# Two GpSimd sums of a fused FFT and two-MLP kernel, issued at the end of earlier rounds

## The chip, the cores and the metric

The kernel runs on one core of one Trainium2 chip. The metric is the device time of one execution in microseconds (us). The core's engines run side by side, each through its own queue of instructions in order: TensorE (PE in the rows, its weight loads PEld), VectorE (DVE), ScalarE (ACT), GpSimd (POOL) and SyncE (SP), which issues most DMAs.

## The reference, cut to what matters

```python
X = np.fft.fft(np.fft.fft(x, axis=1), axis=2).real   # x: 8 x 3072 x 256
h = X.reshape(24576, 256) @ moe_w_in                 # 256 -> 2048
x2 = (h - np.tanh(h)) @ moe_w_out                    # 2048 -> 256
h2 = x2 @ moe2_w_in                                  # 256 -> 1024
e = np.exp(h2 - h2.max(-1)); solu = h2 * e / (e.sum(-1) + 1e-9)
ln = (solu - solu.mean(-1)) / np.sqrt(solu.var(-1) + 1e-6) * g_ln
out = ln @ moe2_w_out                                # 1024 -> 256
```

All of it is in float32. To multiply at TensorE's faster rate with nearly that precision, the kernel splits each operand into a rounded high part and the rest (low part), and makes three passes: high x high, high x low, low x high.

## The kernel before, in words

The transforms over the sequence come first (until about 165 us). The transform over the features is folded into the first weights. What then fills the time is a loop over 48 groups `n` of 512 output rows, with 16 rounds `j` each (`step = 16 n + j`); `m`, a chunk of 128 of the first layer's 2048 features, goes with a round. A round issues work of several ages, in an order that is written out by hand, and each engine executes its share in that order:

- `parity` (L879) makes h of chunk `m` on TensorE, `act_in` (L904, L912) finishes it on VectorE and takes tanh on ScalarE, `act_out` (L921) subtracts; the high part `gh` is rounded by ScalarE (L166) and the low part by GpSimd (`rest`, L169), two rounds after h. One chunk in four has its low part from VectorE instead. `o1` (L941), three rounds after h, multiplies `gh` by the second weights into x2 (`x2p`); its last two of six matmuls read the low part.
- After the last chunk of a group, in round 2 of the next, ScalarE copies x2 (transposed: features x rows) to `xb`: blocks A11, A12, A21, A22. The second layer's first product is made by a Strassen-like scheme of seven products, and so needs sums of blocks, which GpSimd makes in `sum_x2` (L957): S1 = A21 + A22, S2 = S1 - A11, S3 = A11 - A21, S4 = A12 - S2. Each is for both halves (128 rows each) of the group's row pairs.
- `split_x2` splits blocks into high (ScalarE, L166) and low parts (GpSimd, L169) in `xs`, half by half: A11 and A12 in round 3, S2 and S3 in round 5, A22, S1 and S4 in round 7 for the first half; in rounds 11, 13 and 15 for the second.
- `product` (L970) multiplies them into two banks, `bank_a` and `bank_b`. The product of S2 stands at the end of round 6 (second half: round 14): its three passes read the high part twice, and the low part of S2 last.
- The rest of the second layer follows over some 20 rounds: `block` (L992), `power` (L1007), `weigh` (L1016, on VectorE: u times e, both in SBUF), `square` (L1027), `scale` (L1035 to L1041, three small GpSimd instructions), `turn` (L1046, then a transpose through DRAM), `split_moved` (high part on ScalarE, low part `ut` on GpSimd, L169), `outp` (L1074, L1081), `scaled` and `store` (L1095). Two `weigh` fall in rounds 4 and 6, two in 12 and 14; `split_moved` falls in the even rounds.

Within a round the order is: `parity`, `act_in`, `lead`, `act_out` (with `rest` for `gh`), `layer2(step, "ahead")`, the block sums, `layer2(step, "early")` (with `split_moved`, then `split_x2`), `o1`, `layer2(step, "late")`, then weights of the first two groups, loads and sums for the next group.

So GpSimd's order is, in round 3: S1, S2, low part of A11 and A12; in round 4: `gh`, S3, `ut`; in round 5: `gh`, S4, low part of S2 and S3; in round 6: `gh`, then others.

Of the kernel before, what the change touches and what calls it, by code (L numbers as in the profile page):

```python
# [32 lines left out]
NG = B * GPB  # L33
# [106 lines left out]
def fft2_moe_moe_kernel(  # L140
# [559 lines left out]
    for q in range(NQ):  # L700
        b, j = divmod(q, NSJ)
# [73 lines left out]
    A11, A12, A21, A22, S1, S4, S2, S3 = range(8)  # L775
# [22 lines left out]
    def split_wi2(eng, b):  # L798
        split_halves(eng, wi2[:, b, 0], wi2[:, b, 1], whole_of(b))
# [152 lines left out]
    def sum_x2(b):  # L952
        a0, a1, op = {
            S1: (A21, A22, ALU.add), S2: (S1, A11, ALU.subtract),
            S3: (A11, A21, ALU.subtract), S4: (A12, S2, ALU.subtract),
        }[b]
        nc.gpsimd.tensor_tensor(out=xb[:, b], in0=xb[:, a0], in1=xb[:, a1], op=op)  # L957
# [9 lines left out]
    def product(p, bank, a, b, start=False):  # L967

        for q, (hx, hw) in enumerate(PASSES):
            nc.tensor.matmul(  # L970
                in_pairs(bank),
                xs[:, hx, xs_at[a]],
                in_turn(wi2[:, b, hw]),
                start=(start and q == 0),
                stop=(q == 2),
                skip_group_check=True,
            )

    def new_u(t):
        us[t] = (wk.tile([P, FF2], F32, tag="u", bufs=3, name=f"u{t}"), None)  # L980
        sts[t] = wk.tile([P, 12], F32, tag="st", bufs=8, name=f"st{t}")
        return us[t][0]

    def kept(t, f):
        nc.scalar.copy(out=us[t][0][:, f * HF : (f + 1) * HF], in_=bank_b)
# [27 lines left out]
    def weigh(t, h=None):  # L1013
        e, st = es.pop(t), sts[t]
        u = us[t][0]
        nc.vector.scalar_tensor_tensor(  # L1016
            out=u, in0=u if h is None else h, scalar=-1.0 if h is None else 1.0, in1=e,
            op0=ALU.mult, op1=ALU.mult, accum_out=st[:, 2:3],
        )
        us[t] = (u, e)  # L1020
# [72 lines left out]
    def store(t):  # L1093
        o = o2s.pop(t)
        nc.vector.scalar_tensor_tensor(  # L1095
            out=o, in0=pos.pop(t)[:, :D], scalar=sts.pop(t)[:, 10:11], in1=o, op0=ALU.mult, op1=ALU.add
        )
        us.pop(t)
        nc.sync.dma_start(out=out[t * P : (t + 1) * P, :], in_=o)
# [8 lines left out]
    def layer2(step, place):  # L1108

        works = {  # L1110
            "ahead": (
                (20, lambda p: store(2 * p + 1)),
                (24, lambda p: store(2 * p)),
                (2, lambda p: product(p, bank_a, A12, B21)),
                (4, lambda p: product(p, bank_b, S3, T3)),
                (6, lambda p: product(p, bank_b, A22, T4)),
                (1, lambda p: nc.scalar.copy(out=bank_b, in_=bank_a)),
                (3, lambda p: (new_u(2 * p), kept(2 * p, 1))),
            ),
            "early": (  # L1120
                (17, lambda p: outp(2 * p + 1, 0)),
                (19, lambda p: outp(2 * p + 1, 1)),
                (21, lambda p: outp(2 * p, 0)),
                (23, lambda p: outp(2 * p, 1)),
                (3, lambda p: block(2 * p, 0, bank_a, False, True)),
                (5, lambda p: block(2 * p + 1, 1, bank_a, True, True)),
                (6, lambda p: block(2 * p + 1, 0, bank_b, False, False)),
                (7, lambda p: block(2 * p, 1, bank_a, True, False)),
                (7, lambda p: power(2 * p + 1)),
                (8, lambda p: (power(2 * p), weigh(2 * p + 1))),  # L1130
                (9, lambda p: turn(2 * p + 1)),
                (10, lambda p: (weigh(2 * p), square(2 * p + 1), scale(2 * p + 1))),
                (12, lambda p: (square(2 * p), scale(2 * p), turn(2 * p))),
                (14, lambda p: split_moved(2 * p + 1, 0)),
                (16, lambda p: split_moved(2 * p + 1, 1)),
                (18, lambda p: split_moved(2 * p, 0)),
                (20, lambda p: split_moved(2 * p, 1)),
                (-1, lambda p: split_x2(p, A11, A12)),
                (1, lambda p: split_x2(p, S2, S3)),
                (3, lambda p: split_x2(p, A22, S4)),  # L1140
            ),
            "late": (
                (0, lambda p: product(p, bank_a, A11, B11, True)),
                (2, lambda p: product(p, bank_b, S2, T2)),
                (4, lambda p: product(p, bank_a, S1, T1, True)),
                (6, lambda p: product(p, bank_a, S4, B22)),
                (4, lambda p: (new_u(2 * p + 1), kept(2 * p + 1, 1))),
                (19, lambda p: scaled(2 * p + 1)),
                (23, lambda p: scaled(2 * p)),
            ),  # L1150
        }
        for back, work in works[place]:
            p = pair_at(step, back)
            if p is not None:
                work(p)
# [11 lines left out]
    for step in range(steps + 3):  # L1167
        n, j = divmod(step, NM)
        if step in at_ab:
            special(at_ab[step])  # L1170
        if 0 < step <= steps:
            parity(*divmod(step - 1, NM), 1)
        if step < steps:
            even(n, j)
        if 0 < step <= steps:
            act_in(*divmod(step - 1, NM))
        if step < steps:
            lead(n, j)
        lag = 3 if step < NM else 2
        for s in range(out_done, min(step - lag + 1, steps)):  # L1180
            act_out(*divmod(s, NM))
        out_done = max(out_done, min(step - lag + 1, steps))
        if step - 1 in wo2_at:
            split_wo2(wo2_at.index(step - 1), True)
        layer2(step, "ahead")
        if 0 < n < NG:
            for blk in {3: (S1, S2), 4: (S3,), 5: (S4,)}.get(j, ()):
                sum_x2(blk)
        layer2(step, "early")
        if NM <= step < steps + 2:  # L1190
            low_by_vector(*divmod(step - 2, NM))
        if step in at_o1:
            special(at_o1[step])
        if step in (NM, NM + 2):
            mean_wo2((step - NM) // 2)
        if step == NM + 2:
            nc.tensor.matmul(bank_b, wi2[:, B11, 0, :P], wi2[:, B11, 0], start=True, stop=True)
        s1 = step - 5 if step < NM else step - 3
        for s in (range(o1_done, min(s1 + 1, steps))):
            o1(*divmod(s, NM))  # L1200
        o1_done = max(o1_done, min(s1 + 1, steps))
        layer2(step, "late")
        if step in (3, 5, 7, 9):
            c, part = divmod((step - 3) // 2, 2)
            split_wo1(c + 2, wo1_raw[c + 2], slice(part * 2, part * 2 + 2))
        if step == NM:
            raw1.close()
            mv = pool(mv_stack, "mv", 2, side="right")
        if step in wi2_sums:
            sum_wi2(nc.vector, wi2_sums[step])  # L1210
        if step in wi2_splits:
            split_wi2(nc.gpsimd, wi2_splits[step])
        if step in (2, 3):
            load_wo2(step - 2)
        if step == 3:
            for k in range(2):
                load_wi2(k)
        if 8 <= step < NM:
            gain_wo2(step - 8)
        if step in (NM + 3, NM + 4):  # L1220
            center_wo2(step - NM - 3)
        if step in wo2_at:
            split_wo2(wo2_at.index(step), False)
        if step == NM + 12:
            nc.scalar.copy(out=pas, in_=pa)
        if step == NM + 20:
            special_out()
        if n == NG - 1 and j == 9:

            b12 = zp.tile([P, HF], F32, tag="zf", name="b12")  # L1230
            nc.sync.dma_start(out=b12, in_=wi2_d[0][:, HF:])
        if n == NG - 1 and j == 12:
            split_halves(nc.gpsimd, wt[0][:, 0, 0], wt[0][:, 1, 0], b12)
        if step == NM + 30:
            make_identity(nc, ident)
        if 1 <= n and n + 1 < NG:
            if j == 3:
                load_z(n + 1)
            for u in range(2):
                if j == 7:  # L1240
                    sum_z(n + 1, u, nc.gpsimd)
                if j == 11:
                    whole, hi, lo = by_half(n + 1, u)
                    rnd(hi, whole)
                    rest(nc.gpsimd, lo, whole, hi)
# [158 lines left out]
```

## Time and profile before

| | |
|---|---|
| median of 3 runs | 2728.41 us (2728.27 to 2728.82) |
| profiled execution | 2731.39 us |
| its span, first to last instruction | 2729.3 us |
| TensorE busy (matmuls) | 2650.9 us, 97% of the span |
| VectorE busy | 2200.1 us, 81% |
| ScalarE busy | 2035.8 us, 75% |
| GpSimd busy | 2084.7 us, 76% |
| mean granted TensorE clock | 0.997 |

A row of a timeline has the start, the duration, the engine, the line, the instruction with its output and inputs, and in brackets the idle time of the engine just before it, with what ended it. On GpSimd and TensorE the durations are rough; the distance from one start to the next, where the engine doesn't idle, is the better measure of what an instruction takes of its engine.

### The profile page before, as it was taken

The numbers are of one execution on the slowest core, as the hardware profiler recorded it, in microseconds if no ns is written. First come the engines' busy times: TensorE is split into PE (matmuls) and PEld (weight loads), VectorE is DVE, ScalarE is ACT, GpSimd is POOL, SyncE is SP. The second block draws the span as 40 slices with busy tenths as digits, with TensorE's granted clock in tenths as the row PEclk, the third lists the DMA queues.
The fourth block names the chain that finished last, engine by engine and source line by source line (L and its number), as shares of the span: only waits on it lengthen the run. The fifth ranks groups of instructions, "written<-read, shape, count | busy, mean of one in ns | idle before, by whom it ended". The sixth has DMA issues, their size and how long they took to land.

```text
span 2729.3 us, 47917 instructions
## 1 busy us (share of the span) xinstructions
PE 2650.9 (97%) x15073; PEld 2345.3 (86%) x15073; DVE 2200.1 (81%) x4389; ACT 2035.8 (75%) x3990; POOL 2084.7 (76%) x2309
## 2 busy tenths in 40 slices
PE   9999999999999999999999999999999999999998
PEld 6677888888888888888888888888888888888887
DVE  8977788888878888787877888878887788787885
ACT  3556777777777777777777777777777777777775
POOL 0047888888888888888888888888888888888874
PEclk9989999999999999999999999999999999999999
DMA  9951444444444443444444444344444444444441
GB/s 357 367 180 44 101 93 101 100 96 101 99 95 102 100 97 90 107 94 94 103 101 97 96 99 102 93 107 94 95 102 101 99 95 99 101 93 106 94 93 51
DMA packets 882652, 302.99 MB, mean 111 GB/s; under 512 B 788544, under 2 KB 844144, under 8 KB 879104
## 3 DMA queue, kind: packets, MB, share of 16 engines
q1 hardware_dynamic: 879792, 293.45, 43.9%
q10 hardware_dynamic: 2304, 6.42, 0.6%
q8 instruction: 120, 1.97, 0.3%
q14 instruction: 132, 1.08, 0.1%
q0 software_dynamic: 304, 0.07, 0.0%
HBM read 161.26 MB, written 138.60 MB: 110 GB/s over the span
## 4 chain that ended last, share of the span: by engine, by line
PE 74%; POOL 14%; DVE 5%; issue 4%; DMA 2%; ACT 1%; SPq 0%; POOLq 0%; DVEq 0%; ACTq 0%
PE x2p L941 29%; PE h L879 16%; PE po L1074 10%; PE bank_a L970 7%; PE bank_b L970 6%; PE po L1081 5%; POOL gh L169 5%; POOL xs L169 4%; POOL xb L957 3%; POOL ut L169 2%; DVE cv L452 1%; DVE pm L457 1%; DVE sm L447 1%; DMA tts<-tt 0%; DMA x<-xr 0%
## 5 line engine op out<-in xcount | busy, mean ns | idle before, releaser
L941 PE MATMUL x2p<-gh,wo 128*128 128x512 f32 x4608 | 1125.9, 380 | 1.4 <-POOL gh L169 1.4
L169 POOL TENSOR_TENSOR gh<-t,gh 128x512 fp32r<-128x512 f32 x584 | 812.7, 1392 | 257.2 <-ACT gh L166 243.9
L941 PEld LDWEIGHTS x2p<-gh,wo 128*128 128x128 f32 x4608 | 831.0, 190 | 116.2 <-POOL gh L169 10.6
L912 ACT ACTIVATE t<-h 128x512 f32<-128x512 f32 x762 | 453.5, 595 | 368.7 <-DVE h L904 298.5
L904 DVE SCALAR_TENSOR_TENSOR h<-asb,h 128x256 f32<-128x256 f32 x762 | 326.3, 428 | 458.5 <-PE h L879 452.3
L879 PEld LDWEIGHTS h<-zs,wt 128*128 128x128 f32 x4572 | 633.3, 191 | 49.0 <-DVE asb L897 2.9
L879 PE MATMUL h<-zs,wt 128*128 128x256 f32 x4572 | 643.0, 276 | 4.2 <-DVE asb L897 2.1
L1074 PE MATMUL po<-wo,ut 128*128 128x512 f32 x1528 | 522.2, 383 | 1.9 <-DVE o L1095 1.1
L169 POOL TENSOR_TENSOR ut<-um,ut 128x512 fp32r<-128x512 f32 x372 | 477.8, 1284 | 5.1 <-ACT ut L166 5.1
L166 ACT ACTIVATE gh<-t 128x512 fp32r<-128x512 f32 x584 | 370.0, 633 | 139.9 <-DVE t L921 137.0
L1081 PE MATMUL po<-wo,ut 128*128 128x256 f32 x1528 | 416.5, 273 | 0.0
L921 DVE TENSOR_TENSOR t<-h,t 128x512 f32<-128x512 f32 x578 | 395.2, 684 | 0.0
L169 POOL TENSOR_TENSOR xs<-xb,xs 128x256 fp32r<-128x256 f32 (+1 forms) x282 | 279.1, 990 | 133.9 <-ACT xs L166 101.2
L897 DVE SCALAR_TENSOR_TENSOR asb<-nb,wnu,h 128x256 f32<-128x256 f32 x762 | 363.5, 477 | 1.9 <-PE h L879 1.9
L1074 PEld LDWEIGHTS po<-wo,ut 128*128 128x128 f32 x1528 | 289.9, 190 | 32.9 <-DVE o L1095 1.6
L970 PE MATMUL bank_a<-wi,xs 128*128 128x512 f32 x1128 | 305.8, 380 | 1.9 <-POOL xs L169 1.1
L970 PE MATMUL bank_b<-wi,xs 128*128 128x512 f32 x846 | 242.1, 386 | 53.4 <-POOL xs L169 52.7
L1081 PEld LDWEIGHTS po<-wo,ut 128*128 128x128 f32 x1528 | 293.4, 192 | 0.2
L1016 DVE SCALAR_TENSOR_TENSOR u<-u,e 128x1024 f32<-128x1024 f32 x188 | 279.9, 1489 | 0.0
L970 PEld LDWEIGHTS bank_a<-wi,xs 128*128 128x128 f32 x1128 | 206.2, 189 | 28.2 <-POOL xs L169 1.7
L1046 DVE STREAM_TRANSPOSE tb<-u 128x1024 f32<-128x1024 f32 x186 | 229.7, 1235 | 0.0
L166 ACT ACTIVATE ut<-um 128x512 fp32r<-128x512 f32 x372 | 229.3, 616 | 0.0
(156 smaller groups left out, 3161.9 us busy)
## 6 DMA issues: line engine op xcount, KB each, us to landing
mv_d<-tb SPq DMA_DIRECT2D x186, 512.0 KB, 2.7
um<-mv_d SPq DMA_DIRECT2D x744, 128.0 KB, 3.8
out<-o SPq DMA_DIRECT2D x192, 128.0 KB, 1.7
x<-xr SPq DMA_DIRECT2D x23, 1024.0 KB, 10.6
zf<-z_d SPq DMA_DIRECT2D x64, 128.0 KB, 3.7
z_d<-zt ACTq DMA_DIRECT2D x16, 392.0 KB, 6.1
wi<-w_in SPq DMA_DIRECT2D x6, 1024.0 KB, 6.9
z_d<-zt SPq DMA_DIRECT2D x16, 384.0 KB, 9.6
```

The costliest lines, as they stand in the source:

```text
L166: nc.scalar.activation(out=o, in_=i, func=AF.Copy)
L169: eng.tensor_tensor(out=o, in0=i, in1=hi.bitcast(F32), op=ALU.subtract)
L879: nc.tensor.matmul(in_pairs(hs[n, m][:, 0]), wt[c][:, hw, u, o : o + P], in_turn(zs[:, hz, u]), start=(u == 0 and i == 0), stop=(i == 2), ...
L897: nc.vector.scalar_tensor_tensor(out=asb, in0=zg[n][1], scalar=wnu[:, m : m + 1], in1=hs[n, m][:, 0], op0=ALU.mult, op1=ALU.add)
L904: nc.vector.scalar_tensor_tensor(out=h[:, 1], in0=as_.pop((n, m)), scalar=2.0, in1=h[:, 0], op0=ALU.mult, op1=ALU.subtract)
L912: nc.scalar.activation(out=t, in_=h, func=AF.Tanh)
L921: nc.vector.tensor_tensor(out=g, in0=h, in1=t, op=ALU.subtract)
L941: nc.tensor.matmul(in_pairs(x2p[n][mt]), wo1[c][:, hw, k, mt * P : (mt + 1) * P], in_turn(gh[:, hg]), start=(m == 0 and i == 0), stop=(m = ...
L970: nc.tensor.matmul(in_pairs(bank), xs[:, hx, xs_at[a]], in_turn(wi2[:, b, hw]), start=(start and q == 0), stop=(q == 2), skip_group_check= ...
L1016: nc.vector.scalar_tensor_tensor(out=u, in0=u if h is None else h, scalar=-1.0 if h is None else 1.0, in1=e, op0=ALU.mult, op1=ALU.mult, a ...
L1074: nc.tensor.matmul(in_pairs(po), ut[:, 0, ks], wo2[:, k].rearrange("p h x n -> p (x n) h"), start=(k == 0), stop=False,)
L1081: nc.tensor.matmul(in_pairs(po[:, :D]), ut[:, 1, ks], wo2[:, k, :, 0].rearrange("p h n -> p n h"), start=False, stop=(k == NK2 - 1),)
```

## The change

S3 is no longer issued in round 4 behind that round's `gh`, but at the end of round 3, behind the split of A11 and A12. S4 is no longer issued in round 5 behind that round's `gh`, but at the end of round 4, behind `split_moved`. GpSimd's order is then, in round 3: S1, S2, low part of A11 and A12, S3; in round 4: `gh`, `ut`, S4; in round 5: `gh`, low part of S2 and S3. What each instruction computes is as before.

```diff
         layer2(step, "ahead")
-        if 0 < n < NG:
-            for blk in {3: (S1, S2), 4: (S3,), 5: (S4,)}.get(j, ()):
-                sum_x2(blk)
+        if 0 < n < NG and j == 3:
+            sum_x2(S1)
+            sum_x2(S2)
         layer2(step, "early")
...
         layer2(step, "late")
+        if 0 < n < NG and j in (3, 4):
+            sum_x2((S3, S4)[j - 3])
         if step in (3, 5, 7, 9):
```

## Rows read from the trace of the kernel before

**Rows 1.** Waits of TensorE's matmuls: us in total, times, longest.
```profile
PE bank_b L970 <- POOL xs L169: 52.7, 48, 1.2
```
**Rows 2.** Busy time by stretch: one group; from one low-part product to the next.
```profile
1104.00:1156.40 52.40, 51.29 (x300) 46.30 (x299) 42.29 (x86) 40.70 (x80) 43.41 (x49) 1.00 0.43 99
1115.60:1140.79 25.19, 25.19 (x147) 22.88 (x148) 20.06 (x41) 18.54 (x38) 20.98 (x25) 1.00 0.41 95
```
**Rows 3.** Timeline of TensorE around the end of a round 6.
```profile
1112.60 1.46 PE L941 MATMUL x2p<-gh,wo 128*128 128x512 f32 x6
1113.89 0.59 PE L970 MATMUL bank_b<-wi,xs 128*128 128x512 f32 x2
1115.60 0.48 PE L970 MATMUL bank_b<-wi,xs 128*128 128x512 f32 x1 [1.11 <-POOL xs L169]
1115.92 0.83 PE L879 MATMUL h<-zs,wt 128*128 128x256 f32 x6
```
**Rows 4.** The same of that group's round 14.
```profile
1140.79 0.81 PE L970 MATMUL bank_b<-wi,xs 128*128 128x512 f32 x3
1141.44 0.83 PE L879 MATMUL h<-zs,wt 128*128 128x256 f32 x6
```
**Rows 5.** Timeline of GpSimd, rounds 3 to 5 of that group.
```profile
1106.22 0.74 POOL L169 TENSOR_TENSOR xs<-xb,xs 128x256 fp32r<-128x256 f32 x1 [0.63 <-PE h L879]
1108.15 1.86 POOL L169 TENSOR_TENSOR gh<-t,gh 128x512 fp32r<-128x512 f32 x1 [1.19 <-ACT gh L166]
1109.97 0.73 POOL L957 TENSOR_TENSOR xb<-xb 128x256 f32<-128x256 f32 x1
1110.66 1.28 POOL L169 TENSOR_TENSOR ut<-um,ut 128x512 fp32r<-128x512 f32 x1
1111.90 1.28 POOL L169 TENSOR_TENSOR gh<-t,gh 128x512 fp32r<-128x512 f32 x1
1113.14 0.74 POOL L957 TENSOR_TENSOR xb<-xb 128x256 f32<-128x256 f32 x1
1113.83 1.72 POOL L169 TENSOR_TENSOR xs<-xb,xs 128x256 fp32r<-128x256 f32 x1
```
**Rows 6.** Timeline of VectorE: weigh in rounds 4, 6 and 14; what follows in 7.
```profile
1107.65 1.22 DVE L1016 SCALAR_TENSOR_TENSOR u<-u,e 128x1024 f32<-128x1024 f32 x1
...
1113.15 1.81 DVE L1016 SCALAR_TENSOR_TENSOR u<-u,e 128x1024 f32<-128x1024 f32 x1
...
1116.45 0.43 DVE L904 SCALAR_TENSOR_TENSOR h<-asb,h 128x256 f32<-128x256 f32 x1 [1.48 <-PE h L879]
...
1140.05 1.80 DVE L1016 SCALAR_TENSOR_TENSOR u<-u,e 128x1024 f32<-128x1024 f32 x1
```
**Rows 7.** Timeline of ScalarE: high parts of ut, gh and xs.
```profile
1109.11 0.61 ACT L166 ACTIVATE ut<-um 128x512 fp32r<-128x512 f32 x1
...
1110.24 0.63 ACT L166 ACTIVATE gh<-t 128x512 fp32r<-128x512 f32 x1
...
1111.29 0.41 ACT L166 ACTIVATE xs<-xb 128x256 fp32r<-128x256 f32 x1
```
**Rows 8.** Timeline of GpSimd, round 14 of that group.
```profile
1140.04 0.73 POOL L169 TENSOR_TENSOR xs<-xb,xs 128x256 fp32r<-128x256 f32 x1
```
**Rows 9.** Timeline of TensorE: its waits for xs in groups 1 and 2.
```profile
217.15 0.48 PE L970 MATMUL bank_a<-wi,xs 128*128 128x512 f32 x1 [1.05 <-POOL xs L169]
...
224.21 0.48 PE L970 MATMUL bank_b<-wi,xs 128*128 128x512 f32 x1 [0.95 <-POOL xs L169]
...
274.30 0.48 PE L970 MATMUL bank_b<-wi,xs 128*128 128x512 f32 x1 [0.59 <-POOL xs L169]
```
**Rows 10.** Timeline of GpSimd, group 1, round 4.
```profile
217.06 1.27 POOL L169 TENSOR_TENSOR gh<-t,gh 128x512 fp32r<-128x512 f32 x1
```
**Rows 11.** Timeline of GpSimd, group 23, round 5: S4.
```profile
1376.15 1.79 POOL L957 TENSOR_TENSOR xb<-xb 128x256 f32<-128x256 f32 x1
```
**Rows 12.** Timeline of GpSimd, group 18, round 7: sums for the next group.
```profile
1120.45 1.51 POOL L272 TENSOR_TENSOR zc<-zf 128x128 f32<-128x128 f32 x4
```

## The prediction, made before the changed kernel was run

> **What bounds the kernel now.** I read the waits of TensorE first, then the busy time by stretch, then the timelines of the four engines around the wait. TensorE waits for one thing of weight: the low part of S2, at the end of round 6, for which GpSimd is late [rows 1]. In a group of 52.40 us its rows are busy for 51.29, and the 1.11 left is this one wait [rows 2, 3]. The second half of the group, whose round 14 has the same product, shows none: there TensorE is busy for 25.19 of 25.19 us [rows 2, 4]. So what GpSimd loses or gains before this product moves the end, and nothing else on GpSimd does as long as its other results come in time.
>
> The wait costs more than its row says, since the pipe drains and refills. From the start of the product to the next h it is 1115.92 - 1113.89 = 2.03 us in round 6 [rows 3], and 1141.44 - 1140.79 = 0.65 in round 14 [rows 4]: 1.38 us are lost in each such round.
>
> Why is the low part late? GpSimd first idles 1.19 us for the `gh` of round 4, then works without a gap: `gh`, S3, `ut`, `gh`, S4, xs [rows 5]. S4 starts at 1113.14, and weigh, with two operands in SBUF, is issued at 1113.15; it takes 1.81 us and not the 1.22 of 1107.65 [rows 6], so S4 holds it up for 0.59. Then weigh holds up xs, which takes 1.72 instead of the 0.74 of 1106.22, until 1115.55 [rows 5]. TensorE goes on 0.05 later.
>
> **The change part by part.** It adds and removes no instruction; two of a group's four block sums move in GpSimd's queue. None is a DMA, and no DMA queue is passed. In the times of rows 5:
>
> - S3 starts behind the split of A11 and A12, at 1106.22 + 0.69 = 1106.91 (0.69 is the step from S4 to xs, 1113.14 to 1113.83). It reads blocks that are there since before S1, so it waits for nothing. It lies in the idle time that ends at 1108.15, and costs nothing. It is past before the next weigh at 1107.65: that comes 0.74 after it, and a sum holds weigh up for 0.59 only, a margin of 0.15.
> - The `gh` of round 4 keeps its time. Its high part is there at 1108.15, but it lasts 1.86 and not 1.28, as the weigh of 1107.65 runs: in effect it starts at 1108.73, 1.08 after weigh's start. With S3 gone from behind it, `ut` starts at 1109.97; its high part is done at 1109.72 [rows 7], 0.25 before.
> - S4 follows `ut` at 1109.97 + 1.24 = 1111.21, and needs S2 and A12, long done. The `gh` of round 5 then starts at 1111.21 + 0.69 = 1111.90, just when it does now, so the x2 product that reads it loses nothing (its high part is done at 1110.87 [rows 7]).
> - xs starts at 1111.90 + 1.24 = 1113.14, where S4 started; its high part is done at 1111.70 [rows 7]. It takes S4's place in the tie with weigh at 1113.15. If it holds weigh up as S4 did, it ends at 1113.87. TensorE wants it for the third pass, two passes of 0.65 / 3 after 1113.89, so at 1114.32: a lead of 0.45. The wait is gone, and h starts at 1114.54.
>
> Round 14 is this very state already: xs at 1140.04 for 0.73, weigh at 1140.05 for 1.80, the product at 1140.79 without a break [rows 4, 6, 8]. This is the row that I trust for the tie: of 47 groups, 46 have such an xs in round 14, 0.72 to 0.77 long. S4 wins its own tie in all 45 but group 23 [rows 11].
>
> What is late next? weigh ends at 1114.96 as now. VectorE idles 1.48 us behind it for h [rows 6]; 0.10 of that is left, so VectorE just keeps up. The following `gh` is blocked by weigh until about 1114.93 and is 0.58 earlier than now (1113.83 + 1.72 = 1115.55), where TensorE is 1.38 earlier: GpSimd's lead shrinks by 0.80. Round 14 has this too and no wait follows it. What round 15 lacks is the 1.51 us of sums for the next group [rows 12]; I put their cost at 0 (TensorE reads the `gh` behind them three rounds after h) and bound it by 0 and by the whole 1.38.
>
> The sum. Of the 52.7 us in 48 waits [rows 1], 1.05 is for A11 and A12 in group 1, which the change doesn't touch, 0.95 and 0.59 are those of groups 1 and 2 [rows 9], and 50.1 remain for 45 groups, 1.11 each. 45 x 1.38 = 62.1. Group 2 gains 0.59 + 0.27 = 0.86 (0.27 is 1.38 less 1.11). In group 1 GpSimd has no idle time that S3 could fill ([rows 10], and the rows that follow it have none either): the same instructions precede xs, which gains 0, and its `gh` is 0.69 later, so from 0 to -0.7; I take 0, as weights are still being split there. Together 63.0 us, 2.3%: 2731.39 - 63.0 = 2668.4 for the profiled execution, which stands 2.98 above the median; so 2665.4 by the median, 2665.
>
> **The rivals.**
>
> *weigh wins the tie.* xs at 1113.14 and weigh at 1113.15 are as close as they can be. If weigh comes first, it holds xs for 1.08, until 1114.23; xs ends at 1114.96, the third pass starts at 1115.01 and h 0.32 later [rows 3], at 1115.33, which saves 0.59 and not 1.38. For it: group 23, where S4 lost and took 1.79 [rows 11], and that xs, other than S4, has another engine's signal to look at. Against it: round 14 has the same instruction in the same tie and wins. In all 45 groups: 45 x 0.59 + 0.9 = 27, so 2701; each round decides for itself, so anything between. The Trainium skill says the same of the pair ("SBUF — State Buffer", "Who interferes with whom"): a VectorE instruction with two SBUF inputs and a GpSimd one that reads SBUF shut each other out, and the one issued first keeps the ports to its end. The rows agree in kind; by 0.59 of S4's 0.73 the hold is a little shorter than the whole instruction.
>
> *S3 runs into the weigh of round 4.* If S3 comes more than 0.15 later against that weigh, and weigh goes first, S3 waits for it and `gh`, `ut`, S4, `gh` and xs are 0.69 later. The `gh` is then ready at 1113.83, while the fifth x2 matmul wants it at 1112.60 + 4 x 0.216 = 1113.46: about 0.4 of wait and 0.27 of refill, 0.67. xs ends at 1114.96, in time for a product 0.67 later. It saves 0.71 a group, 32 in all: 2697. For it: 0.15 is little. Against it: both stand in a fixed distance to h.
>
> *Something behind the product is late instead*, the lead of 0.80 above being needed: as TensorE has no other wait now, I can't see which; it takes back up to all of it, 2676 to 2728, that is to no change.
>
> *Slower: TensorE's clock.* The wait is TensorE's one break per group. If an engine without it were granted the lower level, 1.2 for 2.4 GHz, in some stretches, each us of work there would cost another. From 63 us of work at the lower level on, the kernel is slower than before; at 90 us it takes 2755. For it: nothing but that no trace shows TensorE this busy for 2 ms. Against it: 25.19 us without a gap at a granted clock of 1.00 [rows 2].
>
> **How the numbers follow.** The forecast (2659 to 2675: at most a quarter of the ties lost, or 0.2 us a group on either side) gets 0.78, weigh's tie 0.09, S3 0.04, a new wait 0.06, the clock 0.03. Range: the forecast's own, and upward into the tie and S3 to 2697, as 0.78 alone leaves a little too much out. What a measurement of this kernel can tell is about 0.2%, 5.5 us. Faster: forecast, tie, S3, and half of the new wait: 0.94. Within: most of the other half, and a little of the clock: 0.03. Slower: 0.03.
>
> **What would show it.** In the timeline of the changed kernel, S3 fills the idle time before the `gh` of round 4; xs of round 5 lasts about 0.73, weigh behind it 1.8; TensorE's waits no longer have the row of xs with 48 times, but 2 or 3; a group takes about 51.0 us. An xs of 1.7 would show the tie lost, a `gh` of round 5 later than now against h the second rival, a new row in TensorE's waits with some 45 times the third, a granted clock under 1.00 in the groups the fourth. The prediction is wrong if a group stays above 51.5 us.

## The result, and the profile after

The changed kernel takes 2669.9 us (median of 4 runs, 2665.96 to 2670.99) where the kernel before takes 2728.61: a ratio of 0.9778, 95% interval 0.9761 to 0.9795. The profiled execution took 2669.49 us, with a span of 2667.7.

The waits of TensorE's matmuls and the busy time by stretch (one group, 51.02 us long), in the kernel after:

```profile
PE bank_b L970 <- POOL xs L169: 3.4, 6, 0.8
```
```profile
1008.06:1059.08 51.02, 51.02 (x299) 46.27 (x298) 42.56 (x88) 40.45 (x81) 42.94 (x49) 1.00 0.43 101
```

This row has fallen from 48 waits to 6 [rows 1]: four in groups that are told of below, and two that the kernel before has as well, in group 1 and in round 14 of group 47. TensorE has no gap left in a group [rows 2]. The granted clock stays at 1.00.

The timelines of GpSimd, VectorE and TensorE in rounds 3 to 7 of one group after, in this order:

```profile
1135.99 0.74 POOL L169 TENSOR_TENSOR xs<-xb,xs 128x256 fp32r<-128x256 f32 x1 [0.63 <-PE h L879]
1136.68 0.74 POOL L957 TENSOR_TENSOR xb<-xb 128x256 f32<-128x256 f32 x1
1137.91 1.88 POOL L169 TENSOR_TENSOR gh<-t,gh 128x512 fp32r<-128x512 f32 x1 [0.50 <-ACT gh L166]
1139.74 1.29 POOL L169 TENSOR_TENSOR ut<-um,ut 128x512 fp32r<-128x512 f32 x1
1140.98 0.74 POOL L957 TENSOR_TENSOR xb<-xb 128x256 f32<-128x256 f32 x1
1141.67 1.28 POOL L169 TENSOR_TENSOR gh<-t,gh 128x512 fp32r<-128x512 f32 x1
1142.92 0.73 POOL L169 TENSOR_TENSOR xs<-xb,xs 128x256 fp32r<-128x256 f32 x1
...
1137.42 1.22 DVE L1016 SCALAR_TENSOR_TENSOR u<-u,e 128x1024 f32<-128x1024 f32 x1
...
1142.91 1.82 DVE L1016 SCALAR_TENSOR_TENSOR u<-u,e 128x1024 f32<-128x1024 f32 x1
...
1144.84 0.43 DVE L904 SCALAR_TENSOR_TENSOR h<-asb,h 128x256 f32<-128x256 f32 x1
...
1143.66 0.81 PE L970 MATMUL bank_b<-wi,xs 128*128 128x512 f32 x3
1144.31 0.83 PE L879 MATMUL h<-zs,wt 128*128 128x256 f32 x6
```

S3, at 1136.68, has taken 0.69 of the 1.19 us that GpSimd idled [rows 5]; 0.50 is left. The `gh` of round 5 starts 5.68 after the xs of round 3, as before, and xs of round 5 now follows it and lasts 0.73 where it lasted 1.72. The product runs as one row of three matmuls, and h follows 0.65 after its start, not 2.03 [rows 3, 4]. weigh is held up by xs now (1.82), as S4 did before [rows 6], and VectorE goes on to h without an idle time where it had 1.48.

So xs and weigh come up for execution at the same moment (a tie, as the prediction calls it), and here xs goes first. In 4 of the 45 groups from group 3 on, weigh does. The same three engines in one of these:

```profile
1091.11 1.80 POOL L169 TENSOR_TENSOR xs<-xb,xs 128x256 fp32r<-128x256 f32 x1
...
1091.11 1.22 DVE L1016 SCALAR_TENSOR_TENSOR u<-u,e 128x1024 f32<-128x1024 f32 x1
...
1091.85 0.59 PE L970 MATMUL bank_b<-wi,xs 128*128 128x512 f32 x2
1092.96 0.48 PE L970 MATMUL bank_b<-wi,xs 128*128 128x512 f32 x1 [0.52 <-POOL xs L169]
1093.29 0.83 PE L879 MATMUL h<-zs,wt 128*128 128x256 f32 x6
```

Both records start at 1091.11; weigh takes its 1.22, xs waits for it, and h comes 1.44 after the start of the product instead of 0.65: 0.79 lost.

### The profile page after: what moved, and what is told of

It reads as the page before. It is cut to its first block, busy times and chain, and to the rows that moved or that the text cites. A ratio compares the mean times of both kernels' runs of the same rounds, so it can differ in the third digit from the quotient of the medians.

```text
span 2667.7 us, 47947 instructions
## 1 busy us (share of the span) xinstructions
PE 2635.9 (99%) x15073; PEld 2343.7 (88%) x15073; DVE 2202.2 (83%) x4389; ACT 2031.4 (76%) x3990; POOL 2079.6 (78%) x2309
## 4 chain that ended last, share of the span: by engine, by line
PE 88%; POOL 2%; DVE 1%; issue 1%; ACT 0%; POOLq 0%; DVEq 0%; ACTq 0%
PE x2p L941 35%; PE h L879 18%; PE po L1074 12%; PE bank_a L970 9%; PE bank_b L970 7%; PE po L1081 6%; POOL gh L169 1%; POOL xs L169 0%; POOL ut L169 0%; POOL xb L957 0%; DVE u L1016 0%; PE ph L1286 0%; DVE t L921 0%; ACT gh L166 0%; PE pt L1303 0%
## 5 line engine op out<-in xcount | busy, mean ns | idle before, releaser
L169 POOL TENSOR_TENSOR gh<-t,gh 128x512 fp32r<-128x512 f32 x584 | 848.9, 1454 | 205.4 <-ACT gh L166 188.7
L897 DVE SCALAR_TENSOR_TENSOR asb<-nb,wnu,h 128x256 f32<-128x256 f32 x762 | 363.4, 477 | 0.6 <-PE h L879 0.6
L169 POOL TENSOR_TENSOR xs<-xb,xs 128x256 fp32r<-128x256 f32 (+1 forms) x282 | 240.2, 852 | 127.9 <-ACT xs L166 96.3
L970 PE MATMUL bank_b<-wi,xs 128*128 128x512 f32 x846 | 230.9, 381 | 4.1 <-POOL xs L169 3.4
```

The costliest lines, as they stand in the source:

```text
L169: eng.tensor_tensor(out=o, in0=i, in1=hi.bitcast(F32), op=ALU.subtract)
L897: nc.vector.scalar_tensor_tensor(out=asb, in0=zg[n][1], scalar=wnu[:, m : m + 1], in1=hs[n, m][:, 0], op0=ALU.mult, op1=ALU.add)
L970: nc.tensor.matmul(in_pairs(bank), xs[:, hx, xs_at[a]], in_turn(wi2[:, b, hw]), start=(start and q == 0), stop=(q == 2), skip_group_check= ...
```

## The experiments

Each was compared with the kernel before on its own chip: the first four with 2727.8 us; the others, on another chip, with 2727.89, and in a later series (the same instruction where there is no tie, and weigh with one operand) with 2729.45. Groups 3 to 46 are timed from the first sum of group 3 to that of group 47 in the profile, which leaves out the start: 2312.8 us before, 2253.9 after.

**S3 alone**

```diff
-            for blk in {3: (S1, S2), 4: (S3,), 5: (S4,)}.get(j, ()):
+            for blk in {3: (S1, S2), 5: (S4,)}.get(j, ()):
...
         layer2(step, "late")
+        if 0 < n < NG and j == 3:
+            sum_x2(S3)
```

> S3 alone is moved to the end of round 3; S4 stays in round 5 behind gh. My theory: what counts is when the low part of S2 and S3 starts on GpSimd against weigh, and S3 alone fills the idle time of 1.19 us before the gh of round 4. The gh of round 5 starts 0.69 us earlier (1111.21 in the times of rows 5), S4 at 1112.45, xs at 1113.14, as with both moves: about 2670 us, some ties with weigh lost. Rival (each move gives its share): about 2699.

2665.19 us (2662.08 to 2668.87), ratio 0.9772 (0.9757 to 0.9787); groups 3 to 46 in 2250.5. As my theory had it: from group 3 on, the move of S3 is the whole gain, and here no tie is lost in these groups. (In group 2, which is taken up below, xs still meets weigh with S4 in front of it, and the group takes 53.85 instead of 53.00.)

**S4 alone**

```diff
-            for blk in {3: (S1, S2), 4: (S3,), 5: (S4,)}.get(j, ()):
+            for blk in {3: (S1, S2), 4: (S3,)}.get(j, ()):
...
         layer2(step, "late")
+        if 0 < n < NG and j == 4:
+            sum_x2(S4)
```

> S4 alone is moved to the end of round 4; S3 stays in round 4 behind gh. My theory: no idle time is filled, so xs keeps its start at 1113.83 (times of rows 5), weigh runs from 1113.15 to 1114.23 ahead of it, xs ends at 1114.96; and the gh of round 5 is 0.69 later, for which the x2 product waits about 0.4 and 0.27 of refill. Saves 0.71 of 1.38 a group: 2696, 2690 to 2702. Rival 1 (it is enough that no sum holds weigh up in round 6): about 2668. Rival 2 (the sum that was behind gh doesn't matter): 2728.

2728.59 us (ten runs, 2724.85 to 2731.0), ratio 1.0001 (0.9992 to 1.001). Nothing is gained; my 2696 was wrong, and so was rival 1. GpSimd, VectorE and TensorE in rounds 5 and 6:

```profile
1057.10 1.29 POOL L169 TENSOR_TENSOR gh<-t,gh 128x512 fp32r<-128x512 f32 x1
1058.33 1.72 POOL L169 TENSOR_TENSOR xs<-xb,xs 128x256 fp32r<-128x256 f32 x1
...
1057.66 1.81 DVE L1016 SCALAR_TENSOR_TENSOR u<-u,e 128x1024 f32<-128x1024 f32 x1
...
1058.44 0.70 PE L941 MATMUL x2p<-gh,wo 128*128 128x512 f32 x2 [0.30 <-POOL gh L169]
1058.97 0.59 PE L970 MATMUL bank_b<-wi,xs 128*128 128x512 f32 x2
1060.10 0.48 PE L970 MATMUL bank_b<-wi,xs 128*128 128x512 f32 x1 [0.54 <-POOL xs L169]
```

I had let weigh run alone. But the `gh` that S4 pushed back is under way when weigh comes, and holds it for the same 0.59; xs is behind weigh as before and takes its 1.72. One wait of 1.11 has become two of 0.30 and 0.54, each with another 0.27 from start to start: 1.38 again. Which GpSimd instruction meets weigh doesn't matter; xs must be in front.

**S3 at the end of round 3, S4 behind xs**

```diff
+        if 0 < n < NG and j in (3, 5):
+            sum_x2({3: S3, 5: S4}[j])
```

(behind `layer2(step, "late")`; S1 and S2 stay in round 3.)

> S3 at the end of round 3 as in the change, but S4 at the end of round 5, behind the split of S2 and S3, which doesn't read it. My theory: xs starts 0.69 earlier than in the changed kernel (1112.45) and weigh at 1113.15 can't come first: no tie is lost, xs never lasts over 1 us in round 5, and the time is that of the change less 0.79 for each lost tie, about 2666, with less spread between runs. Rival (the runs of the change differ for another reason): 2670 and the same spread of 5 us; or, if S4 in weigh's tie holds up what follows, slower than the change by up to 0.59 a group, 2696.

2661.18 us (2660.34 to 2662.43), ratio 0.9757 (0.9743 to 0.9772); groups 3 to 46 in 2250.4, no tie lost. It is the fastest version that ran, by 6 us of medians over the change in the same series, but the intervals overlap, and the next run shows that most of the difference between the two profiles lies before any instruction that was moved.

**The change again**

> The changed kernel itself, on the same chip as the three others: 2666 to 2671, each run by 0.79 us longer for each tie that xs of round 5 loses to weigh. A profile with k such xs of 1.8 us has a span of about 2664.5 + 0.79 k.

2667.18 us (2662.33 to 2669.23), ratio 0.9775 (0.9758 to 0.9793). The profiled execution lost no tie in round 5, and its groups 3 to 46 took 2250.5, like those of the kernel with S4 behind; with four lost ties they took 2253.9. The four groups with a lost tie take 0.78 more than their like (51.80 for 51.02), as the rows above had it, so ties explain 3 us between the two profiles of the change.

The rest of the spread is from before the loop's first sum: that of group 1 starts at 213.55 and 214.59 in the two profiles of the change, at 211.0 with S3 alone, at 210.15 with S4 behind. My guess that the spread comes of the ties was wrong for this larger part of it. The same two engines are at odds there. GpSimd, VectorE and TensorE in the kernel after, and its granted clock behind the wait; then VectorE with S4 behind:

```profile
181.06 1.30 POOL L169 TENSOR_TENSOR gh<-t,gh 128x512 fp32r<-128x512 f32 x1
182.30 1.33 POOL L169 TENSOR_TENSOR wi<-xb,wi 128x512 fp32r<-128x512 f32 x1
183.57 1.28 POOL L169 TENSOR_TENSOR gh<-t,gh 128x512 fp32r<-128x512 f32 x1
184.79 1.31 POOL L169 TENSOR_TENSOR wi<-xb,wi 128x512 fp32r<-128x512 f32 x1
...
181.49 5.15 DVE L795 TENSOR_TENSOR sum_wi<-xb 128x512 f32<-128x512 f32 x1
186.68 0.69 DVE L795 TENSOR_TENSOR sum_wi<-xb,sum_wi 128x512 f32<-128x512 f32 x1
...
188.15 1.01 PE L879 MATMUL h<-zs,wt 128*128 128x256 f32 x3 [4.42 <-DVE asb L897]
```
```profile
187.30:194.10 6.80, 5.96 (x20) 5.32 (x21) 6.09 (x9) 3.70 (x7) 4.21 (x3) 0.50 0.00 0
```
```profile
181.88 1.33 DVE L795 TENSOR_TENSOR sum_wi<-xb 128x512 f32<-128x512 f32 x1
```

A VectorE sum of weights, with two operands in SBUF, is issued while a `gh` is under way. With S4 behind it waits for that one; in the kernel after it waits for four GpSimd instructions in a row, and a like one behind it, with GpSimd idle, takes 0.69. TensorE then idles 4.42 us at once, and its granted clock is 0.50 from 187.3 to 194.1; with S4 behind it idles twice, 1.60 and 1.70, and the clock stays at 1.00. From the first h of the loop to the first sum it takes 53.5 and 53.4 us in the two profiles of the change, and 49.5 with S4 behind. The long sum (5.1) stands in five of the twelve profiles (both of the change, S4 alone at the end of round 4, one small instruction in front of xs, weigh with one operand), and in the other seven it lasts 1.28 to 1.40. All twelve have the same instructions up to there, in the same order on each engine. What decides it, no run shows. The shortest execution of the change, 2662.33, is near what it would take without it (an estimate from these profiles: 2667.06 - 4.0 = 2663).

What the order with S4 behind gains for sure is the tie and 0.7 us in group 1 (46.57 us for 47.27).

**S4 alone, the other way**

```diff
-            for blk in {3: (S1, S2), 4: (S3,), 5: (S4,)}.get(j, ()):
+            for blk in {3: (S1, S2), 4: (S3,)}.get(j, ()):
...
         layer2(step, "late")
+        if 0 < n < NG and j == 5:
+            sum_x2(S4)
```

> S3 stays in round 4 behind gh, as before; S4 alone is moved the other way, to the end of round 5, behind the split of S2 and S3. No idle time of GpSimd is filled before the product. My theory: only the start of xs against weigh counts, and with S4 behind it xs starts at 1113.14 (times of rows 5), in the tie with weigh, as in the changed kernel: about 2670, 2665 to 2675. Rival (the gain comes of issuing the sums sooner, into the idle time): 2728, as both sums are as late as before or later.

2688.89 us (2684.01 to 2689.46), ratio 0.9847 (0.9826 to 0.9869), not the 2670 that I expected. The wait for xs is gone (but for one lost tie) without any sum having been moved forward, so the start of xs is what counts; but 0.56 a group is lost elsewhere. TensorE's waits, then GpSimd and TensorE:

```profile
PE x2p L941 <- POOL gh L169: 12.3, 44, 0.6
```
```profile
1092.45 0.73 POOL L169 TENSOR_TENSOR xs<-xb,xs 128x256 fp32r<-128x256 f32 x1
1093.14 1.71 POOL L957 TENSOR_TENSOR xb<-xb 128x256 f32<-128x256 f32 x1
...
1104.94 2.70 POOL L169 TENSOR_TENSOR gh<-t,gh 128x512 fp32r<-128x512 f32 x2
...
1106.29 0.70 PE L941 MATMUL x2p<-gh,wo 128*128 128x512 f32 x2 [0.28 <-POOL gh L169]
```

S4 now sits behind weigh (1.71), and all that follows on GpSimd is 0.69 later: `gh`, scale, `ut`, xs, the four sums for the next group, `gh`, scale, `ut`, and the `gh` at 1104.94. That is the one TensorE waits for, 13 us behind the cause: 0.28 and another 0.27 from start to start, 44 times. This is the prediction's third rival, come true here. In the changed kernel less than 0.3 of GpSimd's lead is left at that place: the same `gh` runs from 1154.75 for 1.28, and the first matmul that reads it, the fifth of a row that starts at 1155.43, comes at 1155.43 + 4 x 0.216 = 1156.29.

**One small instruction in front of xs**

```diff
     def split_x2(p, b0, b1):
+        if b0 == S2 and p % 2 == 0:
+            nc.gpsimd.tensor_scalar(out=spare, in0=mhalf, scalar1=1.0, scalar2=0.0, op0=ALU.mult, op1=ALU.add)
```

> The changed kernel with one more GpSimd instruction, a product of a 128x1 tile with 1, ahead of the low part of S2 and S3 in each round 5; the small ones of scale show 0.29 us from start to start. My theory: xs then comes behind weigh at 1113.15 in all 45 groups, waits until 1114.23 and costs TensorE 0.79 a group more: about 2702. Rival (weigh and xs share the memory evenly, or xs's lead of 0.45 over TensorE is all that counts): 0.29 is within the lead, so 2670.

2705.11 us (2700.55 to 2706.05), ratio 0.9908 (0.9886 to 0.9929): 35 us more than the change at its first measurement and 38 more than at its second; 2702 was expected. GpSimd, VectorE (weigh is L1019 here) and TensorE:

```profile
1051.27 0.18 POOL L962 TENSOR_SCALAR spare<-mhalf 128x1 f32<-128x1 f32 x1
1051.42 1.69 POOL L169 TENSOR_TENSOR xs<-xb,xs 128x256 fp32r<-128x256 f32 x1
...
1051.27 1.26 DVE L1019 SCALAR_TENSOR_TENSOR u<-u,e 128x1024 f32<-128x1024 f32 x1
...
1053.17 0.48 PE L973 MATMUL bank_b<-wi,xs 128*128 128x512 f32 x1 [0.56 <-POOL xs L169]
```

An instruction that puts xs back by 0.15 costs 0.87 a group (2289.0 in groups 3 to 46, for 2250.5 without a lost tie). All 45 groups lose the tie: in 38 xs waits for weigh, as here, and in 7 the small instruction itself does, which then lasts 1.25 and not 0.18, with xs behind it.

**The same instruction where there is no tie**

(The kernel with S4 behind xs, and the lines of the last diff.)

> The kernel of s4_behind (S3 at the end of round 3, S4 behind the split of S2 and S3) with the same small GpSimd instruction ahead of the low part of S2 and S3 that cost the change 35 us in tie_lost. My theory: xs then starts at 1112.74 in the times of rows 5, still 0.4 ahead of weigh, and TensorE's lead is not touched: the time of s4_behind, 2661, 2659 to 2664. Rival (0.29 of GpSimd's time ahead of the product costs in itself): 45 x 0.29 = 13 more, 2674, or 35 more as there, 2696.

2664.72 us (2662.73 to 2669.65), ratio 0.9771 (0.9753 to 0.9788), just above what I gave and below either rival; groups 3 to 46 in 2252.4, which is 1.9 more than without it. So the small instruction itself costs 0.04 a group; the rest of its price above is the lost tie.

**weigh a round later, in the kernel before**

```diff
-                (10, lambda p: (weigh(2 * p), square(2 * p + 1), scale(2 * p + 1))),
+                (10, lambda p: (square(2 * p + 1), scale(2 * p + 1))),
+                (11, lambda p: weigh(2 * p)),
```

> The kernel before, with the second block's weigh a round later (round 7 and 15 for 6 and 14). GpSimd's order is as before. My theory: xs starts at 1113.83 as before, but nothing holds it: it ends at 1114.57, TensorE's third pass waits 0.28 and refills for some 0.1, and 1.0 of 1.38 is saved: 2683, up to 2700 if weigh in rounds 7 and 15 holds up something else. Rival (weigh has no part in it, the sums alone are late by 0.69): 2728, the wait unchanged.

2836.65 us, ratio 1.0392 (1.0371 to 1.0413), far off. Its GpSimd and VectorE rows, TensorE's, and the waits:

```profile
1093.66 0.75 POOL L169 TENSOR_TENSOR xs<-xb,xs 128x256 fp32r<-128x256 f32 x1
...
1097.26 2.09 DVE L1016 SCALAR_TENSOR_TENSOR u<-u,e 128x1024 f32<-128x1024 f32 x1
...
1099.28 0.68 DVE L169 TENSOR_TENSOR gh<-h,gh 128x512 fp32r<-128x512 f32 x1
...
1100.10 0.57 PE L879 MATMUL h<-zs,wt 128*128 128x256 f32 x3 [1.55 <-DVE gh L169]
```
```profile
PE h L879 <- DVE gh L169: 135.8, 92, 1.6
```

xs lasts 0.75, as I had said, though weigh's place alone was changed. But in rounds 7 and 15 VectorE makes a low part itself, and this also frees the bank of h; weigh now stands in front of it, and TensorE waits 92 times. The run says nothing of the price of weigh in round 6. The next one does.

**weigh with one operand, in the kernel before**

```diff
+        if h is None and t % 2 == 0:
+            nc.vector.transpose(out=u, in_=e)
+            nc.vector.memset(st[:, 2:3], 0.0)
+            us[t] = (u, e)
+            return
```

> The kernel before, with the second block's weigh (rounds 6 and 14) replaced by a 128x1024 transpose of e into u, one operand in SBUF, and a 128x1 memset: the weighting of every even block is left out. GpSimd's order and VectorE's load (1.24 us for 1.22) stay. My theory: xs starts at 1113.83 as before and nothing holds it, so it ends at 1114.55; TensorE's third pass starts at 1114.60 and h at 1114.92 instead of 1115.92: 1.0 saved in each of 45 groups, 2683, 2678 to 2690. Rival (the two sums alone make xs late, or any long VectorE instruction holds it): 2728.

2684.58 us (2681.64 to 2689.45), ratio 0.9838 (0.9821 to 0.9856). The kernel leaves out the weighting of every even block. GpSimd, VectorE and TensorE:

```profile
1098.47 0.73 POOL L169 TENSOR_TENSOR xs<-xb,xs 128x256 fp32r<-128x256 f32 x1
...
1097.79 1.23 DVE L1017 STREAM_TRANSPOSE u<-e 128x1024 f32<-128x1024 f32 x1
...
1098.54 1.21 PE L970 MATMUL bank_b<-wi,xs 128*128 128x512 f32 x3
1099.58 0.61 PE L879 MATMUL h<-zs,wt 128*128 128x256 f32 x4
```

A VectorE instruction as long, with one operand, neither waits for S4 (1.23) nor holds xs (0.73). h comes 1.04 after the start of the product, which is 0.39 more than 0.65; so 1.0 of the 1.38 was weigh's hold on xs, and 0.4 that xs was simply late.

A transpose differs from weigh in more than its operands. The kernel before shows that the operation alone doesn't do it: L897 is a scalar_tensor_tensor like weigh, but takes one operand from SBUF and one from PSUM. Counts and shortest, median and longest duration in ns, from 320 us on, of L897 and of weigh:

```profile
L897 DVE SCALAR_TENSOR_TENSOR asb<-nb,wnu,h x715: 468/478/481, 320.2 to 2667.5; 128x256 f32<-128x256 f32 x179
L1016 DVE SCALAR_TENSOR_TENSOR u<-u,e x181: 1210/1220/1836, 324.2 to 2687.8; 128x1024 f32<-128x1024 f32 x181
```

With GpSimd busy for three quarters of the time, L897 never takes longer than 0.48; weigh does.

**Both sums in round 3**

```diff
+        if 0 < n < NG and j == 3:
+            sum_x2(S3)
+            sum_x2(S4)
```

(behind `layer2(step, "late")`.)

> S3 and S4 both at the end of round 3. S4 would start at 1107.60 (times of rows 5), 0.05 ahead of the weigh of round 4, and hold it for 0.54; that weigh then holds the gh of round 4 until 1109.27. xs starts at 1112.99, 0.15 or more ahead of the weigh of round 6. My theory: VectorE's idle time of 0.46 before the h of round 6 takes most of the delay, no tie is lost: 2665 to 2668. Rival (the second one of the prediction: a sum that runs into the weigh of round 4 costs): the x2 product waits for gh or h, up to 0.7 a group, 2680 to 2700.

2670.28 us (2668.46 to 2673.2), ratio 0.9786 (0.9762 to 0.9811); groups 3 to 46 in 2257.5. No tie is lost, but a group takes 51.12 and not 51.01, so the held weigh of round 4 costs 0.1 (0.4 in 8 groups in which VectorE has one more small instruction): more than I gave it, and far less than the rival did. Nor is it better than the change.

## Why the prediction was right

The 2665 lies 5 us from the median and the measured time in the range; the path through the engines came out as written. Point by point:

- *The place and the price of the wait.* Right: 1.38 a group. Before, an ordinary group takes 52.40 us, after it 51.02. From group 3 to 46, 2312.8 became 2253.9, 58.9 less, and 62.3 less where no tie was lost.
- *S3 fills the idle time, xs takes S4's place, no other instruction moves.* Right to some hundredths of a us in the rows above. That S4 must come sooner too was not claimed, and is not so: S3 alone is enough.
- *weigh's hold.* Shown: an instruction as long with one SBUF operand in weigh's place gave 1.0 back, and 0.15 of delay at the tie costs 0.87. The Trainium skill says as much ("SBUF — State Buffer", "Who interferes with whom"): a VectorE instruction with two SBUF inputs contends with a GpSimd one that reads SBUF, and one with a single SBUF input, outside the two-port modes, does not. The traces agree on both: 1.81 for 1.22 with two, 1.23 with one.
- *The tie.* It was the right rival to fear, and its price was right (0.78 measured, 0.79 given); at 4 of 45 it cost 3.1 us. Two profiles of one kernel differ in it (4 and 0), so how many are lost is luck, as far as these runs show.
- *Group 2.* Here the step failed: I gave it 0.86, and it gained nothing (53.00 us from first sum to first sum, before and after). xs is on time there too, but S3 runs into the weigh of round 4, though not as the second rival had it: S3 goes first. GpSimd, VectorE and TensorE in the kernel after:

```profile
263.72 0.73 POOL L957 TENSOR_TENSOR xb<-xb 128x256 f32<-128x256 f32 x1
...
264.00 1.53 DVE L1016 SCALAR_TENSOR_TENSOR u<-u,e 128x1024 f32<-128x1024 f32 x1
...
266.85 1.25 DVE L860 TENSOR_TENSOR a<-a,pas 128x128 f32<-128x128 f32 x1
...
268.88 1.26 PE L879 MATMUL h<-zs,wt 128*128 128x256 f32 x6 [0.69 <-DVE asb L897]
```

weigh comes 0.28 behind S3 here, not 0.74, and GpSimd holds up VectorE twice: S3 holds weigh, which takes 1.53 and not the 1.22 of before, and the `ut` that now comes sooner holds L860 (two SBUF operands), 1.25 and not 0.70. TensorE waits for VectorE instead. Where S3 stays in round 4 (S4 alone, either way), group 2 takes 52.15 and 52.19: the gain is there, and S3's new place takes it back.
- *The sum.* The profiled execution lost 61.9 us, and 63.0 were forecast. The 45 groups from the third on gave 62.3 and, in group 47, 1.4, so 63.7 where I had 62.1 (1.42 each; I took the commonest round for all); the four ties took 3.1 back, some 0.3 is spread over other groups, and group 2 gave nothing for 0.9. The start happened to be 1.3 earlier (213.55 for 214.87), with no instruction moved in it. That is 61.6 of span. One reading was wrong without harm: the 1.05 of group 1 stands in another row of the waits (`bank_a`), and the 48th wait of [rows 1] is one of 0.54 in round 14 of group 47, which stays.
- *The median.* By medians 58.7 was gained, and most of the 5 us come from here. I took off the 2.98 by which the profiled execution of the kernel before stood above its median; that of the kernel after stands 0.4 below its own. The start differs from one execution to the next. In the profile of the kernel before, TensorE's granted clock was 0.50 for 13.7 us of it; in the kernel after it was 1.00 in that stretch, and the time was lost later, by the long sum of the experiments:

```profile
162.40:176.10 13.70, 13.56 (x57) 12.74 (x57) 6.52 (x14) 6.40 (x11) 6.27 (x5) 0.50 1.04 380
```
- *What is late next.* Nothing, as forecast, but with less to spare than I showed: S4 behind weigh was enough to make a `gh` late four rounds on, where less than 0.3 is left. In the changed kernel TensorE is busy for a whole group.

## What to carry to other kernels

Where two engines shut each other out, the order at the moment of meeting decides, not the amount of work: the same four sums cost 1.38 us a group or nothing. An order that leaves a margin (0.69 with S4 behind xs) loses no tie. Ask of each waiting instruction what is in front of it in its own queue that could have run in an earlier idle time, or could run behind it, as S4 could. A late result can show 13 us behind its cause; look for the whole stretch in which the engine doesn't idle.

## What the runs showed of the hardware that was not expected

- Of two instructions that shut each other out and whose records start within 0.02 us of each other, the GpSimd one mostly went first (33 of 37 groups in one profile of the change, all 37 in the other; in 8 more weigh comes 0.12 later), and with equal starts either could. With the small instruction in front of xs, weigh's record starts 0.02 to 0.05 earlier in 8 groups, and weigh went first in all 8.
- A held VectorE instruction doesn't always go next: one whose like takes 0.69 lasted 5.15, through four GpSimd instructions in a row, where the same one in another profile waited for one.
- A GpSimd instruction holds a VectorE one for 0.59 of its 0.73 us, while VectorE holds GpSimd for 1.08 of 1.22. Even a GpSimd instruction of 0.18, on a 128x1 tile, is held (1.25).
- A wait in the middle of a chain of matmuls costs TensorE some 0.27 us more than its row shows, in the rows of xs and `gh` above.
